# A spectral filter and a GeGLU layer on one core: forward transforms on two 64-row halves of TensorE, filter planes on both partition halves, filter sums made in the inverse's accumulation, and a new order

## The chip, the cores and the metric

The kernel runs on one core of a Trainium2 chip. The core has five engines that run side by side and wait for each other through semaphores: TensorE (matrix products into PSUM), VectorE, ScalarE, GpSimd and SyncE. Sixteen DMA engines move data; transfers are issued from the queue of an engine, here SyncE's and GpSimd's, in the order of that queue. The metric is the device time of one execution in microseconds, from the program's first to its last instruction and what lies around it. Before the change it is 491.61 us, the median of 3 runs (491.15 to 492.12).

## The reference

One sequence of 2,048 rows with 576 features, bfloat16. A spectral filter with a layer norm ahead of it, then a GeGLU layer with another:

```python
def _A_ref(x, w_r, w_i):
    B, S, D = x.shape
    X = rfft2(x.astype(float32), axes=(-2, -1))
    X = X * (w_r + 1j * w_i)          # 2048 x 289 filter
    return irfft2(X, s=(S, D), axes=(-2, -1)).astype(bfloat16)

def _B_ref(x, w_gate, w_up, w_down):  # 576 x 4608, 576 x 4608, 4608 x 576
    return (_gelu(x @ w_gate) * (x @ w_up)) @ w_down

h = x + _A_ref(_layernorm(x), A_w_r, A_w_i)
h2 = h + _B_ref(_layernorm(h), B_w_gate, B_w_up, B_w_down)
```

## The kernel before

There is no transform instruction: each step of the Fourier transform is a matrix product with a table of sines and cosines. The rows are kept as 16 tiles `XO[:, c, :]` of 128 partitions. The work runs in five stages; the order inside the first three is written out by hand as a list of short words, which the builder turns into instructions one after the other, so each engine gets its instructions in the order of the list. `Prog` puts in the semaphore waits from what each instruction reads and writes.

*Stage A* (list `SEQ1`). Statistics of the first layer norm (`B`, `b`, `S`, `Q`, `v`, `q`, `c`), scaled tables `ATS` (`x`, L506 and L511), negated and copied columns of x for the even and odd parts (`n`, `t`: `XN`, L553 and L558), then the first transform over 128 of the 2,048 rows (`M`, `a_mm`, L537) into PSUM, and evictions to `U` (`E`, `F`, L548). `U` holds five column blocks for 16 groups.

*Spectral stage* (list `SEQF`). It works through 16 groups of frequencies, group 1 first, group 0 last (`GORD`). For each group:

- `D` (`st_D`, L611): the transform along the features, six matmuls of 128 rows by 288 columns into two PSUM banks, evicted to `CUS` by ScalarE.
- `B` (`st_B`, L621): the last part of the row transform, four matmuls of 288 columns into two banks, real and imaginary part; evicted to `YS` by ScalarE (L603 is the helper that records all these evictions).
- `T` (`st_T`, L630): VectorE multiplies both parts with both filter planes and a negated one, 4 x 288 products into `TP`.
- `w` (`st_w`, L635): VectorE makes the negated plane, in four pieces.
- `Z` (`st_Z`, L641 and L644): VectorE adds the products pairwise into `ZS` (256 columns) and `ZR` (the 32 columns that remain).
- `V` (`st_V`, L651): the first step of the inverse, four matmuls of 256 columns, evicted to the tile `V` by ScalarE.
- `R` (`st_R`, L663 and L666): the same for the remaining columns, four groups at a time; VectorE multiplies with a mask `MK` into `VR`.

The filter planes lie in `WS`. Partitions 0 to 63 hold the rows of a frequency and 64 to 127 those of its mirror. They come by 22 transfers on SyncE's queue (`w_up`, `w_down`, L441 to L451), the imaginary plane first, with the table `VT` between the two halves; behind them in the same queue come `DT`, `IT`, `DP`, `ITD`, `IDT` and the up weights. The source of a `w_up` steps 16 x 4 x a contiguous run, that of a `w_down` 16 x 8 (or 7) rows of 289 elements, backwards.

*Inverse stage* (list `SEQ`). For the first six tiles, the remaining feature transform (`I`, L736), the row transform (`N`, L779) and the residual (L796), then the second layer norm, transposes (L841) and the first pieces of the GeGLU layer (`g`, `h`). The other ten tiles are done later, between the matmuls of the first down projection (L895, L913).

*GeGLU layer*. Four blocks of 512 rows: gate and up products on two 64-row halves of TensorE (L877), then the down product (L978). The weights for its first quarter are loaded into slot 0 of `WG3`; slots 1 and 2 share memory with `WS`, so their loads wait until the last product `T` is done. The gate half is issued on GpSimd's queue behind all that GpSimd has to do up to there, the up half on SyncE's.

Of the kernel before, what the change touches and what calls it, by code (L numbers as in the profile page):

```python
# [4 lines left out]
BF16 = mybir.dt.bfloat16  # L5
# [5 lines left out]
KW = 288  # L11
HK = 144
NZ = 5
# [10 lines left out]
SEQ1 = """S3 B0 t1 b0 b1 B1 v0 q0 c0 Q3 n0 m3D B2 k14 t0 x0P b2 n1 v1 q1 n2 k104 c1 B5 S4 m4P b5 Q4 B6 M0 E1A b6 v2 B7 x1P E0A M1 E4A q2 E5A t2 b7 c2 B9 E3A x2P E2A E8A E6A b8 S13 B8 b9 v3 q3 k202 M2 B11 B10 n3 n4 c3 x3P E12A b10 b12 E9A b11 B12 v4 E13A Q13 E7A q4 E10A t3 E11A B15 m13P E14A M3 t4 c4 E15A E16A b14 x4P M4 B14 b15 t5 v5 E17D q5 E18A E21A n5 E19A c5 x5D E20D E22D E23A E24A F23A F24A M5 E27A E25D E29A F29A E26D E28D F28A F25D F27D F22A F26D""".split()  # L24
# [3 lines left out]
SEQF = """D0 D1 w0 D2 B0 T0 D3 B1 Z0 D4 T1 Z1 B2 V0 T2 B3 D5 T3 B4 D6 w1 Z2 T4 Z3 D7 B5 D8 w3 B6 w2 D9 T5 Z4 B7 Z5 T6 B8 R0 D11 T7 V2 Z7 D10 V1 B9 T8 B10 D13 Z6 V4 T9 T10 R1 D12 V3 Z8 B11 B12 Z9 D14 T11 V6 B13 T12 V5 B14 Z11 V7 Z10 T13 D15 Z12 T14 V8 Z13 V9 B15 Z14 R2 T15a V12 V10 T15b Z15a V11 Z15b V13 V14 R3 V15 R4""".split()  # L28
VENG = [('act',), ('act',), ('act',), ('act',), ('act',), ('act',), ('act',), ('act',), ('act',), ('act',), ('act',), ('act',), ('act',), ('act',), ('act',), ('act', 'act')]
DENG, BENG = ['act', 'act', 'act', 'act', 'act', 'act', 'act', 'act', 'act', 'act', 'act', 'act', 'act', 'act', 'act', 'act'], ['act', 'act', 'act', 'act', 'act', 'act', 'act', 'act', 'act', 'act', 'act', 'act', 'act', 'act', 'act', 'act']  # L30
SEQ = """I0 I1 N0 I2 s0 N1 I3 S1 q0 N2 I4 c0 e0 s2 q1 n0 n1 N3 I5 c1 z0 n2 s3 e1 D1 N4 N5 e2 q2 c2 n3 e3 D2 g10 g00 h10 z3 h00 g20 g01 h20 h01 g21 g11 h21 h11""".split()
# [14 lines left out]
def build_tables():  # L46
# [39 lines left out]
    fr = np.zeros((6, 128, 2, HK))  # L86
    for o, kk in enumerate((k2o, k2e)):
        for h, fn in enumerate((np.cos, np.sin)):
            for t in range(2):
                fr[3 * o + t, :, h] = fn(ang(np.arange(128 * t, 128 * t + 128), kk))  # L90
            fr[3 * o + 2, 64:96, h] = -fn(ang(np.arange(544, 576), kk))
            fr[3 * o + 2, 96:128, h] = fn(ang(np.arange(256, 288), kk))
# [43 lines left out]
    T["BTAB"] = B.reshape(2, 3, 128, 128).transpose(2, 0, 1, 3).reshape(128, -1)  # L136
    T["VTAB"] = V.reshape(2, 2, 128, 256).transpose(2, 0, 1, 3).reshape(128, -1)
# [175 lines left out]
def _build(nc, A_x, A_w_r, A_w_i, B_w_gate, B_w_up, B_w_down, out):  # L313
# [16 lines left out]
    WS = sb.alloc("WS", [128, 3, NG, K2], BF16)  # L330
# [11 lines left out]
    XN = sb.alloc("XN", [128, NT, 320], BF16)  # L342
# [23 lines left out]
    U = sb.alloc("U", [128, 5, NG, NT, 8], BF16)  # L366
# [7 lines left out]
    FT = sb.alloc("FT", [128, 6, 2 * HK], BF16)  # L374
    BT = sb.alloc("BT", [128, 2, 3, 128], BF16)
    VT = sb.alloc("VT", [128, 2, 2, 256], BF16)
# [4 lines left out]
    assert sb.off <= end1  # L381
# [10 lines left out]
    TP = sb.alloc("TP", [128, 3, 2, 2, KW], BF16)  # L392
    ZS = sb.alloc("ZS", [128, NZ, 2, 256], BF16)
    ZR = sb.alloc("ZR", [128, 2, 2, 128], BF16)

# [42 lines left out]
    def w_up(pl, hf):  # L438
        g0, g1 = ((0, 9), (9, 16))[hf]
        src = (A_w_r, A_w_i)[pl].tensor  # L440
        P.dma(SP, WS[0:64, 1 + pl, g0:g1, :].rearrange("p g k -> p (g k)"), bass.AP(src, g0 * K2, [[128 * K2, 16], [16 * K2, 4], [1, (g1 - g0) * K2]]),  # L441
              f"w{pl}{hf}", w=[("W", hf, pl, 0)])
# [10 lines left out]
    for pl in (1, 0):  # L453
        w_up(pl, 0)
        w_down(pl, 0)
# [593 lines left out]
```

## Time and profile before

The profiled execution took 489.2 us from its first to its last instruction; the median of the runs is 491.61. Busy times and idle times below are of that one execution.

| engine | busy us | share of the span | instructions |
|---|---|---|---|
| TensorE, matmul | 481.8 | 98% | 4,376 |
| TensorE, weight load | 286.3 | 59% | 4,376 |
| VectorE | 193.6 | 40% | 399 |
| ScalarE | 150.7 | 31% | 297 |
| GpSimd | 32.1 | 7% | 60 |

Where it stands in time:

| stage | from, us | to, us |
|---|---|---|
| stage A | 0 | 19.9 |
| spectral stage | 19.9 | 48.3 |
| inverse, second norm, transposes | 48.3 | 57.1 |
| GeGLU, with the last ten inverse tiles inside | 57.1 | 487.3 |

Transfers (of DMA queue records):

| transfer | KB each | issue to landing, us |
|---|---|---|
| FT | 432 | 10.1 |
| BT | 192 | 10.0 |
| WS, eight largest groups | 36 to 325 | 6.1 to 9.6 |
| gate weights | 1,152 | 10.2 |
| output | 72 | 1.6 |

Over the whole span the DMA engines moved 31.2 MB; q1, SyncE's hardware queue, 18.6 MB of it.

How to read it: the busy share of TensorE over the whole span says little about the spectral stage, because the GeGLU layer fills most of the time. What the spectral stage costs is read from that stage alone. In the lines that follow, L611 and the like are lines of the kernel before; an entry such as `x96 | 13.9, 286` is a count, the busy time in us, and the mean time of one in ns. A matmul's recorded time covers its whole way through the array; successive ones overlap, so their spacing, not their mean time, is what they cost TensorE.

### The profile page before, as it was taken

The numbers are of one execution on the slowest core, as the hardware profiler recorded it, in microseconds if no ns is written. First come the engines' busy times: TensorE is split into PE (matmuls) and PEld (weight loads), VectorE is DVE, ScalarE is ACT, GpSimd is POOL, SyncE is SP. The second block draws the span as 40 slices with busy tenths as digits, with TensorE's granted clock in tenths as the row PEclk, the third lists the DMA queues.
The fourth block names the chain that finished last, engine by engine and source line by source line (L and its number), as shares of the span: only waits on it lengthen the run. The fifth ranks groups of instructions, "written<-read, shape, count | busy, mean of one in ns | idle before, by whom it ended". The sixth has DMA issues, their size and how long they took to land.

```text
span 489.2 us, 9939 instructions
## 1 busy us (share of the span) xinstructions
PE 481.8 (98%) x4376; PEld 286.3 (59%) x4376; DVE 193.6 (40%) x399; ACT 150.7 (31%) x297; POOL 32.1 (7%) x60
## 2 busy tenths in 40 slices
PE   7899999999999999999999999999999999999998
PEld 3787754444688744444577644444677544444775
DVE  6799733433576634433311144333211233333111
ACT  6999742233322223323200032233100122323000
POOL 5511441000000020000000000000000000000000
PEclk9999999999999999999999999999999999999999
DMA  8990999100001071100000001000000000000000
GB/s 283 231 325 16 365 366 340 26 15 2 1 19 40 13 233 23 24 4 1 2 18 19 13 20 22 16 0 1 7 19 19 7 1 0 1 2 1 13 20 18
DMA packets 25148, 31.20 MB, mean 64 GB/s; under 512 B 11440, under 2 KB 17840, under 8 KB 25104
## 3 DMA queue, kind: packets, MB, share of 16 engines
q1 hardware_dynamic: 22208, 18.62, 13.4%
q0 software_dynamic: 2896, 11.95, 7.0%
q8 instruction: 34, 0.56, 0.5%
q14 instruction: 10, 0.08, 0.1%
HBM read 26.22 MB, written 2.36 MB: 58 GB/s over the span
## 4 chain that ended last, share of the span: by engine, by line
PE 92%; ACT 3%; DVE 3%; DMA 1%; issue 0%; SPq 0%; POOL 0%; DVEq 0%
PE PS L877 57%; PE PS L978 29%; PE PS L537 1%; DMA XO<-in_A_x_dram 1%; DVE TP L630 1%; PE PS L895 1%; ACT V L603 1%; PE PS L736 1%; ACT YS L603 1%; PE PS L611 1%; PE PS L779 1%; PE PS L913 1%; ACT U L548 0%; DVE VR L666 0%; ACT CUS L603 0%
## 5 line engine op out<-in xcount | busy, mean ns | idle before, releaser
L877 PE MATMUL PS<-HT,WG 64*128 64x512 bf16 (+1 forms) x2160 | 228.7, 371 | 0.0
L877 PEld LDWEIGHTS PS<-HT,WG 64*128 64x128 bf16 x2160 | 105.0, 94 | 121.9 <-issue 0.7
L886 DVE TENSOR_TENSOR AT<-GL,PS 128x512 bf16<-128x512 bf16 (+1 forms) x147 | 99.4, 677 | 177.9 <-ACT GL L885 177.9
L885 ACT ACTIVATE GL<-PS 128x512 bf16<-128x512 f32 (+1 forms) x147 | 86.5, 588 | 262.6 <-PE PS L877 251.3
L978 PE MATMUL PS<-WD,AT 128*128 128x288 bf16 (+2 forms) x1152 | 144.9, 286 | 0.0
L978 PEld LDWEIGHTS PS<-WD,AT 128*128 128x128 bf16 x1152 | 110.7, 98 | 30.6 <-ACT GL L885 0.8
L877 PE MATMUL PS<-HT,WGX 64*128 64x512 bf16 x486 | 53.4, 376 | 0.0
L981 DVE TENSOR_TENSOR OS<-PS,XO 128x288 bf16<-128x288 f32 (+2 forms) x32 | 14.6, 457 | 94.4 <-PE PS L978 94.3
L877 PEld LDWEIGHTS PS<-HT,WGX 64*128 64x128 bf16 x486 | 23.7, 94 | 28.8
L611 PE MATMUL PS<-FT,U 128*128 128x288 bf16 x96 | 13.9, 286 | 0.0
L630 DVE TENSOR_TENSOR TP<-YS,WS 128x1152 bf16<-128x1152 bf16 (+2 forms) x17 | 12.0, 719 | 2.7 <-ACT YS L603 2.5
L900 ACT ACTIVATE EB<-PS 128x288 f32<-128x288 f32 x10 | 4.1, 411 | 27.6 <-PE PS L895 27.6
L537 PE MATMUL PS<-ATS,XO 128*128 128x128 bf16 x96 | 8.6, 219 | 3.1 <-POOL ATS L506 1.6
L480 DVE BATCH_NORM_STATS2 ST<-XO 128x6 f32<-128x288 bf16 x26 | 10.0, 441 | 2.7 <-DMA XO<-in_A_x_dram 2.7
L918 DVE TENSOR_TENSOR XO<-PS,XO 128x576 bf16<-128x576 f32 x10 | 7.6, 756 | 8.0 <-PE PS L913 8.0
L611 PEld LDWEIGHTS PS<-FT,U 128*128 128x128 bf16 x96 | 9.2, 98 | 2.3
L603 ACT ACTIVATE CUS<-PS 128x576 bf16<-128x576 f32 x16 | 10.4, 659 | 0.5 <-PE PS L611 0.3
L603 ACT ACTIVATE YS<-PS 128x576 bf16<-128x576 f32 x16 | 10.3, 664 | 0.4 <-DVE TP L630 0.4
L621 PE MATMUL PS<-CUS,BT 128*128 128x288 bf16 x64 | 10.0, 286 | 0.0
L548 ACT ACTIVATE U<-PS 128x256 bf16<-128x256 f32 (+2 forms) x29 | 9.6, 417 | 0.7 <-PE PS L537 0.6
L906 DVE TENSOR_TENSOR QB<-PS,EB 128x288 f32<-128x288 f32 x20 | 8.2, 452 | 3.3 <-ACT EB L900 3.3
L823 DVE TENSOR_SCALAR HN<-XO,NM,RS 128x576 bf16<-128x576 bf16 (+1 forms) x28 | 9.2, 369 | 0.1
(80 smaller groups left out, 207.6 us busy)
## 6 DMA issues: line engine op xcount, KB each, us to landing
WD<-in_B_w_down_dram POOLq DMA_DIRECT2D x9, 576.0 KB, 12.0
WG<-in_B_w_up_dram SPq DMA_DIRECT2D x4, 1152.0 KB, 7.8
WG<-in_B_w_gate_dram POOLq DMA_DIRECT2D x4, 1152.0 KB, 10.2
out_dram<-OS SPq DMA_DIRECT2D x30, 72.0 KB, 1.6
XO<-in_A_x_dram SPq DMA_DIRECT2D x3, 576.0 KB, 7.4
WGX<-in_B_w_up_dram SPq DMA_DIRECT2D x1, 1152.0 KB, 6.0
WGX<-in_B_w_gate_dram POOLq DMA_DIRECT2D x1, 1152.0 KB, 10.0
HT<-HN SPq DMA_TRANSPOSE x60, 2.4
```

Of the source, the lines that this page charges most:

```text
L480: P.op(DVE, lambda v: v.bn_stats(ST1[:, c, h, :], XO[:, c, 288 * h:288 * h + 288]), r=[("X", c)], w=[("ST1", c, h)])
L537: P.op(PE, lambda t, b=b, lhs=lhs, s=s, e=e, o=o, c=c: t.matmul(bank(b, 0, 128, o, o + 128), lhs, ATS[:, c, :], start=s, stop=e), r=[("X", ...
L548: fn = (lambda v: v.tensor_copy(dst, src)) if eng == DVE else (lambda a: a.activation(dst, src, ACTF.Copy))
L603: fn = (lambda v: v.tensor_copy(dst, src)) if eng == DVE else (lambda a: a.activation(dst, src, ACTF.Copy))
L611: P.op(PE, lambda t, b=b, m=m, us=us, o=o: t.matmul(bank(b, 0, 128, 0, 2 * HK), U[:, us, i, :, :], FT[:, 3 * o + (2 if us == 4 else us // ...
L621: P.op(PE, lambda t, b=b, tb=tb, m=m, s3=s3, sp_=sp_: t.matmul(bank(b, 0, 128, 0, KW), BT[:, sp_, tb, :], CUS[:, s3, m, :], start=(m == 0) ...
L630: P.op(DVE, lambda v: v.tensor_tensor(TP[:, tl, :, :, q0:q1], y4, w4, op=ALU.mult), r=[("Y", sl), ("Wn", i)] + (wkeys[0] if 1 <= g < 9 els ...
L877: op = P.op(PE, lambda t, h0=h0, kt=kt, wt=wt, b=b, s=(not second and j == 0), e=(second and j == n - 1): t.matmul(bank(b, 0, 128, c0, c1) ...
L885: P.op(ACT, lambda a: a.activation(GL[:, s2, c0:c1], bank(b0, 0, 128, c0, c1), ACTF.Gelu_apprx_tanh), r=[("PS", b0)], w=[("GL", s2)])
L886: P.op(DVE, lambda v: v.tensor_tensor(AT[:, f, c0:c1], GL[:, s2, c0:c1], bank(b0 + 1, 0, 128, c0, c1), op=ALU.mult), r=[("GL", s2), ("PS", ...
L978: P.op(PE, lambda t, b=b, d0=d0, d1=d1, f=f, p=p: t.matmul(bank(b, 0, 128, 0, d1 - d0), AT[:, f, 128 * p:128 * p + 128], WD[:, f, d0:d1], ...
L981: P.op(DVE, lambda v, b=b, d0=d0, d1=d1, p=p, c=c: v.tensor_tensor(OS[:, p % 2, d0:d1], bank(b, 0, 128, 0, d1 - d0), XO[:, c, d0:d1], op=A ...
```

## The change

Filter planes. `WS` becomes `[128, 2, 2, NG, K2]`: plane, half `h` of a group's frequencies, group, feature. The 64 rows of a half and the mirror rows now lie on partitions 0 to 63, and the same values once more on 64 to 127. They come in four chunks of groups, each chunk in twelve loads from device memory and then two copies from one partition half to the other; the negated plane is gone.

```diff
-    def w_up(pl, hf):
-        g0, g1 = ((0, 9), (9, 16))[hf]
-        P.dma(SP, WS[0:64, 1 + pl, g0:g1, :]..., bass.AP(src, g0 * K2, [[128 * K2, 16], [16 * K2, 4], [1, (g1 - g0) * K2]]),
...
+    WP = ((1, 5), (5, 9), (9, 16), (0, 1))
+    def w_load(j):
+        g0, g1 = WP[j]
+        n = g1 - g0
+        for pl in range(2):
+            src, nm = (A_w_r, A_w_i)[pl].tensor, f"w{pl}{j}"
+            for h in range(2):
+                P.dma(SP, WS[0:32, pl, h, g0:g1, :].rearrange("p g k -> p (g k)"), bass.AP(src, (g0 + 32 * h) * K2, [[16 * K2, 2], [128 * K2, 16], [1, n * K2]]),
+                      nm, w=[("W", pl, j, h)])
+            for jl in range(2):
+                for h in range(2):
+                    p0, k0 = 32 + 16 * jl, 128 - 32 * h - 16 * jl - g0 - 64 * (g0 + jl + h == 0)
+                    P.dma(SP, WS[p0:p0 + 16, pl, h, g0:g1, :], bass.AP(src, k0 * K2, [[128 * K2, 16], [-K2, n], [1, K2]]), nm, w=[("W", pl, j, 2 + 2 * jl + h)])
+    def w_copy(j):
+        g0, g1 = WP[j]
+        for pl in range(2):
+            P.dma(SP, WS[64:128, pl, :, g0:g1, :]..., WS[0:64, pl, :, g0:g1, :]..., f"v{pl}{j}",
+                  r=[("W", pl, j, i) for i in range(6)], w=[("W", pl, j, 6)])
+    w_load(0)
+    w_load(1)
+    w_copy(0)
+    P.dma(SP, VT...)
+    w_load(2)
+    w_copy(1)
+    w_load(3)
+    w_copy(2)
...
+    w_copy(3)
```

Transforms on halves. `U` is laid out so that the 64 lower and the 64 upper partitions of a `D` product hold two halves of the group. `st_D` makes ten matmuls of 64 rows where it made six of 128, in two passes (`D`, six, and `d`, four), so that each pair works on both halves of TensorE and on two banks; the eviction follows the second pass, on ScalarE or, for six groups, on VectorE. `st_B` makes four matmuls of 64 rows.

```diff
+        for j in range(3 - second):
+            for half in range(2):
+                o = half ^ second
+                us, h0, b = (1 - o, 3 - o, 4)[j], 64 * half, b0 + o
+                ... t.matmul(bank(b, 0, 128, 0, 2 * HK), U[h0:h0 + 64, us, i, ...], FT[h0:h0 + 64, ...], start=(not second and j == 0), stop=(second and j == 1))
...
+        for m in range(2):
+            for half in range(2):
+                h0 = 64 * half
+                ... t.matmul(bank(b0 + half, 0, 128, 0, KW), BT[h0:h0 + 64, sp_, m, :], CUS[h0:h0 + 64, s3, m, :], start=(m == 0), stop=(m == 1))
```

Products and sums. `T` multiplies `YS`, or for four groups (word ending in `x`) the PSUM banks directly, with both planes. The sums of `Z` are gone: `V` and `R` accumulate the products in PSUM, with twice as many matmuls of 128 columns that write every other run of four columns. `Z` is now a copy of the 32 remaining columns of the four products, on GpSimd for ten groups, on VectorE for four, on ScalarE for two. `TP` has six buffers where it had three.

```diff
+        w4 = WS[:, :, :, g, 1:K2].rearrange("p w h k -> p h w k")
+        y4 = y.unsqueeze(2).to_broadcast([128, 2, 2, KW])
+        P.op(DVE, lambda v: v.tensor_tensor(TP[:, tl, :, :, :], y4, w4, op=ALU.mult), r=rk + wkeys[3 if g == 0 else (g > 4) + (g > 8)], w=[("T", tl)])
...
+            for h in range(2):
+                for w in range(2):
+                    ... t.matmul(bank(b, ...).rearrange("p (a s e) -> p a s e", s=2, e=4)[:, :, h, :],
+                                 TP[:, tl, h, w, c:256:2], VT[:, sp_, w, h, :], start=(w == 0), stop=(w == 1))
```

Tables and stage A. `FT` goes from 1,728 to 1,440 elements a partition, `BT` from 768 to 512, `VT` stays at 1,024. `XN` holds 256 columns a tile, and a new tile `XR` of 128 takes the tail columns twice, once from each half. Three of the six groups of `ATS` are now scaled on VectorE, one before.

Order. `SEQ1`, `SEQF` and `SEQ` are new lists. The beginning of the spectral one:

```diff
-SEQF = """D0 D1 w0 D2 B0 T0 D3 B1 Z0 D4 T1 Z1 B2 V0 T2 B3 D5 T3 B4 ..."""
+SEQF = """D0 D2 d0D D1 d2 d1D D3 B0x d3 D4 B1x T0x d4 B2 T1x D5 B3 T2 d5 Z0D D7 T3 B4 ... T14 B15 V11 T15 V10 Z13P Z14D V13 R2 Z15 V14 V12 V15 R4 R3"""
```

The wait of the first gate weight load on GpSimd is now for the second chunk of the planes (`wkeys[1]`). The GeGLU layer's code is as before.

More of the change, by code (lines that the diff above doesn't have):

```diff
@@ L12 @@
 HK = 144
-NZ = 5
+NP = 6
 ABASE = 1
@@ L380, in _build @@
     YB = sb.alloc("YB", [128, D], BF16)
-    assert sb.off <= end1
     v_off = max(end1, sb.off)
@@ L697, in _build @@
     wdv = B_w_down[:, :].rearrange("(c p) d -> p c d", p=128)
-    P.alias(wkeys[0] + wkeys[1] + [("Wn", i) for i in range(NG)], [("WG", j, k) for j in (1, 2) for k in range(4)])
+    P.alias(sum(wkeys, []), [("WG", j, k) for j in (1, 2) for k in range(4)])
     def wg_tile(slot):
```

213 lines of the change are left out of this document (96 added, 117 removed).

## The prediction

> **What bounds the kernel now.** I read four views, in this order: the chain of waits in order of time, the busy time by stretch, the groups of instructions by shape, and the DMA view of the first 30 us.
>
> ```profile
> 24.02 0.75 PE PS L611 x6
> ...
> 45.46 2.74 ACT V L603 x6
> ...
> 48.34 1.63 PE PS L736 x12
> ...
> 56.86 0.28 PE PS L841 x5
> ...
> 58.77 0.03 issue
> 58.81 0.44 PE PS L841 x5
> 59.25 68.58 PE PS L877 x674
> ...
> 170.66 70.04 PE PS L877 x648
> ```
>
> Columns: start, length, what. From 59.25 us on, the chain is TensorE alone, gap by gap closed; the change leaves that code as it is. So the change can only act between 0 and 59 us, and what it shifts there shifts the end one for one. The spectral stage runs from the first L611 (20.1) to the inverse (L736, 48.34), some 28.3 us.
>
> ```profile
> core 0: us, PE busy (x) PEld busy (x) DVE busy (x) ACT busy (x) POOL busy (x), PEclk, DMA share, GB/s
> 25.00:30.00 5.00, 5.00 (x43) 4.04 (x42) 4.75 (x12) 4.89 (x9) 1.54 (x2) 1.00 1.05 377
> 30.00:35.00 5.00, 5.00 (x44) 4.10 (x43) 4.93 (x12) 4.58 (x9) 0.00 (x0) 1.00 1.04 331
> 40.00:45.00 5.00, 5.00 (x45) 4.08 (x43) 4.89 (x15) 5.00 (x11) 0.00 (x0) 1.00 0.01 3
> ```
>
> Three engines are full at once in that stage (clock 1.00), so a gain needs all three relieved. The prices:
>
> ```profile
> L630 DVE TENSOR_TENSOR TP<-YS,WS 128x1152 bf16<-128x1152 bf16 x15 | 11.2, 755 | 2.7 <-ACT YS L603 2.5
> L603 ACT ACTIVATE CUS<-PS 128x576 bf16<-128x576 f32 x16 | 10.4, 659 | 0.5 <-PE PS L611 0.3
> L666 DVE TENSOR_TENSOR VR<-PS,MK 128x1024 bf16<-128x1024 f32 x3 | 3.7, 1219 | 0.0
> ```
>
> And the transfers from 5 to 30 us, in 40 slices of 0.625 us, with the issues of the filter planes on SyncE's queue (ns: least/median/most):
>
> ```profile
> GB/s 295 383 339 276 304 390 397 407 401 433 397 420 279 199 243 222 254 222 219 212 224 208 279 215 226 224 229 201 174 192 293 216 255 386 408 403 402 379 407 379
> ...
> L223 SPq DMA_DIRECT2D WS<-in_A_w_i_dram x11: 552/600/706, 5.7 to 16.1; - x11
> L223 SPq DMA_DIRECT2D WS<-in_A_w_r_dram x11: 595/598/612, 9.1 to 20.0; - x11
> ```
>
> About 400 GB/s until slice 12 (12.5 us: x and tables), then about 220 while the filter planes come in, half of them as rows of 578 B. 400 over 16 DMA engines is 25 GB/s each, 220 is 14. The first filter product (L630) starts at 23.62 and waits for ScalarE, not for these transfers.
>
> **The change part by part: the engines.** TensorE: L611's six matmuls of 288 columns take 0.75, 0.122 each, and L621's the same. L877 shows halves of 64 rows: 70.04/648 = 0.108 for 512 columns, so 0.061 for 288. Forward transforms: 96 x 0.122 = 11.7 before, 160 halves x 0.061 = 9.8 after. B: 64 x 0.122 = 7.8 before, 64 x 0.061 = 3.9 after. The inverse's first step (V, R): 74 x 0.11 of 256 columns before, 148 of 128 columns after; L537 does 128 columns in 0.055, so nothing changes, 8.1. Its output now goes in runs of four; no row has that, bounds 0.055 and 0.11 (as 256 columns), I take the first. Sum 27.7 to 21.8.
>
> The 64-row and 128-row forms alternate eight times in the new order, never in the stage before. Between L877's halves five L841 transposes took 0.44, without such neighbours 0.28: 0.08 a switch, 0.6 in all, on an engine that has room. The Trainium skill (TensorEngine Tiling (Array Packing), Key Properties) says that a switch of tiling drains TensorE; a drain of a whole L877 matmul (371 ns) would make it 3 us, the row says 0.6.
>
> ScalarE (spacing back to back 0.55 for 128x576, 0.46 for V): ten CUS of 16, twelve YS of 16, 16 V, two ZR: 20.0 against 25. VectorE loses the sums ZS (16 x 0.34) and the negated plane (L635, 1.8); sixteen ZR sums become copies, ten on GpSimd, four here. It gains six CUS evictions (0.66, as L796 has for 576 from PSUM) and four products read straight from PSUM: VR needs 1.21 for 1,024 such elements, so 1.36 for 1,152 (bounds 0.67 and 2 x 0.75). Sum: 12 x 0.67 + 4 x 1.36 + 6 x 0.66 + 0.5 + VR 5.0 = 23. Begun at 21, that ends at 44 instead of 48.6, where VectorE's last VR ends now. So the engines alone would give up to 4.6 us.
>
> **The filter transfers.** The products of the first four steps now wait for chunk 0 of the planes, the next four for chunk 1, steps 8 to 14 for chunk 2, the last for chunk 3. Each chunk first comes to partitions 0 to 63 in twelve loads, and then goes by two copies to 64 to 127; SyncE's queue runs load 0, load 1, copy 0, VT, load 2, copy 1, load 3, copy 2, copy 3, and only then DT, IT and the weights. A copy waits in that queue for its chunk's landing, and everything behind it too. 22 issues become 56.
>
> Bytes: the up rows are 2 planes x 2 x 32 partitions x 16 x 578 = 1.18 MB, the down rows as many, and the copies 2.37 MB that did not exist. Now the doubtful point. Every transfer of the profile has 16, 64 or 128 entries in the slowest step of both its sides. The sixteen up loads alone break this: source 2 x 16 x n, destination 32 partitions. If the work is dealt out along that step, two DMA engines carry each up load, the other fourteen none. The bounds are 16 and 2; I take 2, since an equal deal along both outermost steps (2 and 32) allows no more. The Trainium skill (DMA: Bandwidth & Descriptors, "How many engines (k)") says that such a DMA is split by the largest k up to 16 that divides both slowest dimensions, on the lowest-numbered engines. No run shown so far can confirm it.
>
> Then each of these two engines carries, up to copy 2: up rows 592 KB, down rows 74, copies 139, VT 16. Long rows at 25 GB/s: 747/25 = 29.9 us; the 578 B rows at 14: 5.3. They start at 12.1 (12.5 less 136 KB of FT and BT no longer loaded). Queue order gives copy 0 at 12.1 + 11.8 + 2.6 + 1.5 + 1 for landing = 29, chunk 1 at 44, chunk 2 at 12.1 + 35.2 + 1 = 48.3. SyncE's issues (24 x 0.64 to 21.1, the next fourteen to 32) lie before that and cost nothing. The landing of 1 us is from the output stores (1.6 from issue, 0.33 of it issuing).
>
> From 48.3, VectorE still has six products of 0.67, two of 1.36, a ZR copy 0.2 and three VR of 2.5 together: 9.4, in order, so the last VR ends at 57.7 against 48.6. All the engines' savings, and the reordered first stage, are hidden behind the planes: step 0 waits until 29 where stage A ends near 20, and 9 us of cover is there.
>
> GpSimd's issue of the first gate weights moves behind ten ZR copies, the last after the thirteenth product (53.7); landing took 10.2, so 64, and the first use comes at 57.1 + 9.1 = 66. Hidden; without that cover, in a stage that ends as before, it would be 47.2 + 10.2 against 57.1, some 0.3 us. DT and IT go out at about 47 and land some 7 later, before 57.
>
> Sum: 9.1 on the profiled execution's 489.2 is 498.3. The median of the runs shown, 491.61, stands 2.4 above that span, so 500.7, say **501**.
>
> **Rivals.** *Dealt to all 16 engines: the queue bounds.* 2.37 MB at 220 and as much at 400 GB/s take 17 us, done by 30; SyncE is the limit. At 0.64 an issue chunk 2's copies leave at 41 and land at 43.3, the stage ends near 53.7: +5.1, 496.7. With the table loads' issue (0.43 + 0.04) for the 32 short loads, they land at 37.8 and the stage ends at 47.2: -1.4, 490.2. Middle 494. For it: 16 DMA engines were busy on all former loads. Against: none of those had a 2 there.
>
> *No plane is late* (faster): copies pass quickly and issues are short; then the engine sums decide: -4.6 with about half a us of gaps given back, 487.5. For it: three engines lose 3 to 6 us each. Against: 34 more issues on one queue at 0.43 or more are 15 us, and the last copy would have to land by 33.
>
> *Two engines at the crowded rate*: long rows at 14 GB/s too make 821/14 = 58.6 us; chunk 2 lands at 71.7, +32.5, 524. For it: the slices around 220. Against: there all sixteen engines worked on rows of 578 B, here fourteen idle most of the time.
>
> **How the numbers follow.** Forecast 0.62, its own range 496 (everything at 433/16 = 27 GB/s, 30.4 us, +4) to 512 (long rows near 18); queue-bound 0.23; no plane late 0.07; crowded rate 0.08. The range 490 to 511 leaves out the last two and little else. A difference of 0.2% (1 us) can be told from none. Faster: 0.07 plus the low end of the queue case, 0.11. Same: 0.08. Slower: 0.81.
>
> **What would show it.** Right: L652, the changed kernel's product, idles before its steps 0, 4 and 8 until about 29, 44 and 48, its releaser a DMA on WS; the copies of WS land long after issue; GB/s in slices from 14 to 45 us falls below 100, as two engines at 25 give; TensorE shows gaps. The queue case would show gates at 24, 34 and 38 to 43 with SyncE issuing without a pause. Wrong altogether: products back to back from 23 us, and the stage's end at 44. L629 halves above 0.07 each, or V matmuls at 0.11, would show my TensorE prices wrong without moving the sum.

## The result, and the profile after

| | before | after |
|---|---|---|
| median of the runs, us | 491.87 (491.15 to 492.31) | 514.32 (512.52 to 515.15) |
| ratio, 95% interval | 1 | 1.0462 (1.0436 to 1.0487) |
| span of the profiled execution, us | 489.2 | 510.7 |
| first filter product (step 0) starts, us | 23.62 | 33.56 |
| last VR ends, us | 48.6 | 69.8 |
| inverse (I) starts, us | 48.34 | 69.51 |

The change makes the kernel 4.6% slower, and all of it is there before the inverse starts: 69.51 − 48.34 = 21.2 of the 21.5 us. Line numbers are now those of the changed kernel: L234 issues a DMA, L629 is `D`, L642 `B`, L652 the product `T`, L659 `V`, L677 and L680 `R`, L619 an eviction, L748 the inverse, L889 the GeGLU products.

First the page's 40 slices of 12.8 us each. Busy tenths of TensorE, the share of the DMA engines in tenths, and what they moved:

```profile
PE   7824799999999999999999999999999999999998
...
DMA  8533989961000107010000001100000000000000
GB/s 278 126 75 82 244 293 349 372 221 22 1 1 13 33 24 225 20 24 1 1 1 18 17 16 25 22 6 1 1 19 17 13 1 1 1 1 1 13 19 17
```

The third and fourth slice (25.5 to 51 us) show TensorE at 2 and 4 tenths, which was full there before, and 75 and 82 GB/s, where the rows of before had 377 and 331 from 25 to 35 us. Who waits for whom is in VectorE's timeline (start, length, instruction; in brackets how long VectorE had idled and what released it):

```profile
33.56 2.62 DVE L652 TENSOR_TENSOR TP<-PS,WS 128x1152 bf16<-128x1152 f32 x2 [9.79 <-DMA WS<-WS]
...
52.17 1.44 DVE L652 TENSOR_TENSOR TP<-YS,WS 128x1152 bf16<-128x1152 bf16 x2 [11.65 <-DMA WS<-WS]
...
57.83 2.36 DVE L680 TENSOR_TENSOR VR<-PS,MK 128x1024 bf16<-128x1024 f32 x2 [1.35 <-PE PS L677]
60.11 1.46 DVE L652 TENSOR_TENSOR TP<-YS,WS 128x1152 bf16<-128x1152 bf16 x2
...
67.41 2.41 DVE L680 TENSOR_TENSOR VR<-PS,MK 128x1024 bf16<-128x1024 f32 x3
```

Step 0 starts at 33.56 and step 4 at 52.17, each after some 10 us of idling, released by a copy within `WS`. Step 8 starts at 60.11 without waiting for its planes, which had landed at 59.1, a microsecond before VectorE was through with what stands ahead of it. The last VR ends at 69.82. The chain of waits (start, length, what) says the same from the other end:

```profile
29.90 5.95 SPq L234
...
38.03 14.07 DMA WS<-WS
52.17 0.77 DVE TP L652
...
53.67 2.10 PE PS L629 x16
...
60.08 0.61 PE PS L629 x10
...
69.51 1.63 PE PS L748 x12
```

One copy takes 14.07 us from its issue to its landing, and ahead of it SyncE spends 5.95 us in a single issue that has a median of 0.43. And the busy time by stretch, for two stretches in which VectorE waits and for the ten microseconds around steps 4 to 8 (the last three numbers of a row are granted clock, share of the DMA engines, GB/s):

```profile
core 0: us, PE busy (x) PEld busy (x) DVE busy (x) ACT busy (x) POOL busy (x), PEclk, DMA share, GB/s
32.00:33.00 1.00, 0.00 (x0) 0.00 (x0) 0.00 (x0) 0.00 (x0) 0.00 (x0) 0.50 0.13 25
44.00:48.00 4.00, 0.00 (x0) 0.00 (x0) 0.00 (x0) 0.00 (x0) 0.00 (x0) 0.88 0.15 54
...
50.00:55.00 5.00, 1.33 (x12) 0.77 (x14) 2.83 (x5) 1.30 (x2) 0.76 (x1) 0.50 0.59 126
55.00:60.00 5.00, 5.00 (x68) 3.78 (x64) 3.65 (x6) 4.01 (x7) 0.30 (x1) 0.77 0.97 234
```

A share of 0.13 is two engines of sixteen, and some 50 GB/s is what two give at 25 each. (The 25 GB/s of the first row is half of that: the packets of copy 0 and VT that were under way there, of 2,312 and 2,048 B, took about 200 ns each; 94 and 84 ns are their times elsewhere. Why is open.) The trace's records of single packets and landings show the two streams directly. Worked out from them, in us from the span's start (the forecast's column from its own terms: long rows at 25 GB/s, short ones at 14, from 12.1 on, 1 us for a landing; chunk 2's rows are 12.1 + 608/25 + 69/14 + 1, with 608 KB of up rows, copy 0 and VT and 69 of down rows on each of the two engines):

```
landed, us                 forecast   after
load 0                       20.3      21.2
load 1                       27.5      31.0
copy 0                       29        33.5
load 2 (rows of chunk 2)     42.4      50.3
copy 1                       44        52.1
copy 2                       48.3      59.1

marks left by one load of a plane: 70 (before: 80 for five transfers, 16 each)
a packet of 4,046 B: 158 ns in two streams alone, 371 ns (median) from 38 to 42 us
a packet of 2,312 B:  94 ns in two streams alone
```

A load of one plane is six transfers and would leave 6 x 16 = 96 marks on its semaphore. It leaves 70 = 4 x 16 + 2 x 3: the four down loads are carried by sixteen engines, the two up loads leave three marks each. The Trainium skill (DMA: Bandwidth & Descriptors, "How many engines (k)") says that the number of engines must divide the slowest dimension of both sides, here 2 and 32; the trace agrees.

### The profile page after: what moved, and what is told of

Read it like the earlier page. It is cut to its first block, busy times and chain, and to the rows that moved or that the text cites. A ratio compares the mean times of both kernels' runs of the same rounds, so it can differ in the third digit from the quotient of the medians.

```text
span 510.7 us, 10214 instructions
## 1 busy us (share of the span) xinstructions
PE 482.7 (95%) x4513; PEld 283.4 (55%) x4514; DVE 192.1 (38%) x376; ACT 146.7 (29%) x288; POOL 36.7 (7%) x68
## 4 chain that ended last, share of the span: by engine, by line
PE 87%; SPq 7%; DMA 3%; ACT 2%; DVE 1%; issue 1%; DVEq 0%
PE PS L889 55%; PE PS L990 28%; SPq L234 7%; DMA WS<-WS 3%; PE PS L629 1%; PE PS L907 1%; PE PS L659 1%; ACT V L619 1%; PE PS L642 0%; PE PS L925 0%; PE PS L748 0%; DVE XO L808 0%; ACT YS L619 0%; ACT OS L782 0%; ACT GS L619 0%
## 5 line engine op out<-in xcount | busy, mean ns | idle before, releaser
L889 PE MATMUL PS<-HT,WG 64*128 64x512 bf16 (+1 forms) x2160 | 228.7, 371 | 0.0
L889 PEld LDWEIGHTS PS<-HT,WG 64*128 64x128 bf16 x2160 | 104.7, 94 | 122.2 <-issue 0.7
L889 PE MATMUL PS<-HT,WGX 64*128 64x512 bf16 x486 | 53.4, 376 | 0.0
L889 PEld LDWEIGHTS PS<-HT,WGX 64*128 64x128 bf16 x486 | 23.7, 94 | 28.8
L629 PE MATMUL PS<-FT,U 64*128 64x288 bf16 x160 | 15.9, 333 | 19.8 <-DVE TP L652 10.0
L629 PEld LDWEIGHTS PS<-FT,U 64*128 64x128 bf16 x160 | 8.0, 107 | 24.7 <-DVE TP L652 10.3
L619 ACT ACTIVATE YS<-PS 128x576 bf16<-128x576 f32 x12 | 7.7, 657 | 21.4 <-PE PS L642 11.2
L652 DVE TENSOR_TENSOR TP<-YS,WS 128x1152 bf16<-128x1152 bf16 x12 | 9.0, 769 | 12.0 <-DMA WS<-WS 11.7
L554 PEld LDWEIGHTS PS<-ATS,XO 128*128 128x128 bf16 x96 | 6.8, 98 | 5.0 <-POOL ATS L523 2.9
L652 DVE TENSOR_TENSOR TP<-PS,WS 128x1152 bf16<-128x1152 f32 x4 | 5.3, 1348 | 9.8 <-DMA WS<-WS 9.8
## 6 DMA issues: line engine op xcount, KB each, us to landing
WG<-in_B_w_up_dram SPq DMA_DIRECT2D x4, 1152.0 KB, 12.7
```

What stands on the lines that cost most here:

```text
L554: P.op(PE, lambda t, b=b, lhs=lhs, s=s, e=e, o=o, c=c: t.matmul(bank(b, 0, 128, o, o + 128), lhs, ATS[:, c, :], start=s, stop=e), r=[("X", ...
L619: fn = (lambda v: v.tensor_copy(dst, src)) if eng != ACT else (lambda a: a.activation(dst, src, ACTF.Copy))
L629: d_done[i, o] = P.op(PE, lambda t, b=b, us=us, h0=h0, o=o, s=(not second and j == 0), e=(second and j == 1): t.matmul(bank(b, 0, 128, 0, ...
L652: P.op(DVE, lambda v: v.tensor_tensor(TP[:, tl, :, :, :], y4, w4, op=ALU.mult), r=rk + wkeys[3 if g == 0 else (g > 4) + (g > 8)], w=[("T", ...
L889: op = P.op(PE, lambda t, h0=h0, kt=kt, wt=wt, b=b, s=(not second and j == 0), e=(second and j == n - 1): t.matmul(bank(b, 0, 128, c0, c1) ...
```

## The experiments

**1. Sixteen engines for the up rows.** Only the cut of the up loads changes: each takes 16 partitions and both halves h, so that the slowest step of both sides is 16. Same number of transfers, bytes and queue order.

```diff
-            for h in range(2):
-                P.dma(SP, WS[0:32, pl, h, g0:g1, :]..., bass.AP(src, (g0 + 32 * h) * K2, [[16 * K2, 2], [128 * K2, 16], [1, n * K2]]),
+            for jl in range(2):
+                P.dma(SP, WS[16 * jl:16 * jl + 16, pl, :, g0:g1, :]..., bass.AP(src, (g0 + 16 * jl) * K2, [[128 * K2, 16], [32 * K2, 2], [1, n * K2]]),
```

> The up loads of the filter planes are cut the other way: one load for each 16 partitions, both halves h in it, so that source and destination both step 16 first. Number of loads, bytes, order of the queue, copies and all compute stay the same. Theory (an up load whose slowest source step is 2 is carried by two of the 16 DMA engines, which then hold up the copies behind it): the copies of chunk 0, 1 and 2 land near 24, 31 to 34 and 38 to 43 us instead of 33.5, 52.1 and 59.1; SyncE issues without stalls of several us; the stage's last VR ends at 47 to 54 instead of 69.8; time 490 to 497. Rival (the copies between partition halves themselves, and the waits for them in SyncE's queue, are what is slow, however the loads are dealt): chunk 1 still lands after 48 and the time stays above 506.

Measured: 498.80 us (498.06 to 499.63), ratio 1.0146 (1.0128 to 1.0164), just above the 490 to 497 that I expected. So 15.5 of the 22.5 us go with this cut alone, and a load leaves 96 marks. VectorE's timeline again:

```profile
25.55 2.62 DVE L652 TENSOR_TENSOR TP<-PS,WS 128x1152 bf16<-128x1152 f32 x2 [1.68 <-DMA WS<-WS]
...
35.27 1.43 DVE L652 TENSOR_TENSOR TP<-YS,WS 128x1152 bf16<-128x1152 bf16 x2 [3.47 <-DMA WS<-WS]
...
45.69 2.23 DVE L652 TENSOR_TENSOR TP<-YS,WS 128x1152 bf16<-128x1152 bf16 x3 [2.23 <-DMA WS<-WS]
```

The waits have shrunk from 9.8 and 11.7 us to 1.7, 3.5 and 2.2, but there are three, all on copies. The two engines are the main cause; some 7 us have another.

**2. No plane is late.** Four long loads of all 128 partitions, from the memory of the gate weights, stand in for planes and copies; the engines' work is that of the change.

```diff
-        for pl in range(2):
-            src, nm = (A_w_r, A_w_i)[pl].tensor, f"w{pl}{j}"
...
+        P.dma(SP, WS[:, :, :, g0:g1, :]..., bass.AP(B_w_gate.tensor, g0 * K2, [[4 * NG * K2, 128], [NG * K2, 4], [1, n * K2]]),
...
     def w_copy(j):
+        return
```

> The filter is left out: WS is filled by four long loads (one for each chunk, 128 partitions, runs of 4 x 578 B and more) from the memory of the gate weights, as many bytes as loads and copies together, so the products are of other numbers; everything else is the changed kernel. It shows what the engines alone make of the new order. Theory (engine sums 22 for TensorE, 20 for ScalarE, 23 for VectorE from 21 us on): no product waits for a plane after about 25 us, the last VR ends at 44 to 46 against 48.6 before, time 486.5 to 489.5. Rival (the new order, eight changes between 64 and 128 rows on TensorE, and V's output in runs of four are slow by themselves): the last VR ends after 48 and the time is above 491.

Measured: 489.17 us (488.86 to 489.48), ratio 0.9950 (0.9933 to 0.9966). The chain of waits ahead of the first product, and from step 4 to 8 VectorE's timeline:

```profile
21.42 2.02 PE PS L619 x29
...
23.47 0.64 DVE CUS L609
...
24.15 1.37 DVE TP L642
```

```profile
24.15 2.62 DVE L642 TENSOR_TENSOR TP<-PS,WS 128x1152 bf16<-128x1152 f32 x2
...
28.89 1.42 DVE L642 TENSOR_TENSOR TP<-YS,WS 128x1152 bf16<-128x1152 bf16 x2
...
36.78 1.50 DVE L642 TENSOR_TENSOR TP<-YS,WS 128x1152 bf16<-128x1152 bf16 x2
```

The engines are worth 2.6 us by the medians (1.8 by the profiled spans, 489.2 and 487.4), not the 4.6 of my sum. Step 0 starts at 24.15, behind the first 29 half matmuls and an eviction, and not at 21. From step 4 (28.89) to step 8 (36.78) it is 7.9 us. The changed kernel took as long (52.17 to 60.11), but that is a coincidence: it had done part of TensorE's work ahead, while VectorE waited, so that 78 matmuls begin in that stretch of its trace and 130 in this one. On the other hand its granted clock was 0.50 when step 4 began (rows above).

**3. The rate by partitions.** As experiment 2, but chunk 0 comes by loads to 64 partitions, chunk 1 by loads to 16, chunks 2 and 3 by loads to 128; the same source.

```diff
+        for p in range(0, 128, np_):
+            P.dma(SP, WS[p:p + np_, :, :, g0:g1, :]..., bass.AP(B_w_gate.tensor, (4 * p * NG + g0) * K2, [[4 * NG * K2, np_], [NG * K2, 4], [1, n * K2]]),
...
+    w_fill(0, 64)
+    w_fill(1, 16)
...
+    w_fill(2, 128)
+    w_fill(3, 128)
```

> The filter is left out again: WS is filled from the memory of the gate weights with the same runs as in the run with free planes, but chunk 0 by two loads of 64 partitions, chunk 1 by eight loads of 16 partitions, chunks 2 and 3 by one load of 128 partitions each. All go out on 16 engines. Theory (a transfer that touches few partitions is limited at the memory side, not by the number of DMA engines: the run with up loads on 16 engines moved only 120 to 220 GB/s while it filled 16 or 64 partitions at a time): a run of 2,312 B takes near 175 ns in chunk 0 (about 210 GB/s in all) and 300 ns or more in chunk 1 (about 110 GB/s), and a run of 4,046 B in chunk 2 about 160 ns (400 GB/s). Rival (the slow rates come from the 578 B rows, or from odd addresses of the filter in device memory): all three chunks move at 370 to 420 GB/s, 2,312 B in 93 ns.

One run of 490.72 us beside 490.79 before: nothing waits for these loads. The busy time by stretch has loads to 64 partitions in its first row, to 16 mostly in the second, to 128 in the third:

```profile
core 0: us, PE busy (x) PEld busy (x) DVE busy (x) ACT busy (x) POOL busy (x), PEclk, DMA share, GB/s
14.00:18.00 4.00, 3.17 (x49) 2.83 (x48) 3.37 (x16) 3.24 (x10) 3.28 (x6) 0.94 1.04 188
22.00:26.00 4.00, 3.91 (x62) 3.01 (x59) 3.45 (x9) 2.23 (x7) 0.00 (x0) 1.00 1.05 174
28.00:32.00 4.00, 4.00 (x68) 3.10 (x66) 3.77 (x7) 4.00 (x10) 1.85 (x3) 1.00 1.01 398
```

All sixteen engines are busy in each, yet they move 174 to 188 GB/s into 16 or 64 partitions and 398 into 128. The packets of 2,312 B took some 200 to 210 ns into 16 partitions as well as into 64, so the 300 ns that I expected for 16 was wrong. The Trainium skill (SBUF — State Buffer, Door 1: The DMA port swizzle) says that partitions 0 to 63 lie on eight of sixteen ports and measured 196 GB/s there; the trace agrees, with 188. So a transfer into one half of the partitions runs at about half rate when sixteen engines carry it; two engines alone still reach 25 GB/s each (2,312 B in 94 ns). For the copies within `WS` the same is read off other traces: in the changed kernel a packet of 2,312 B of a copy took 94 ns (median) on two engines alone from 49 to 52 us, and 171 ns from 22 to 24 us, with the other fourteen on it; copy 0's last packets, around 32 us, are the exception named above.

**4. Steps over partitions, fewer waits.** Rows permuted so that a load steps over every second partition, sixteen engines, chunks of 5, 4, 4 and 3 groups, one copy for both planes.

```diff
-    WP = ((1, 5), (5, 9), (9, 16), (0, 1))
+    WP = ((0, 5), (5, 9), (9, 13), (13, 16))
...
+                P.dma(SP, WS[jl:32:2, pl, :, g0:g1, :]..., bass.AP(src, (g0 + 16 * jl) * K2, [[128 * K2, 16], [32 * K2, 2], [1, n * K2]]),
...
+                    P.dma(SP, WS[32 + jl:64:2, pl, h, s0:g1, :], bass.AP(src, (128 - 32 * h - 16 * jl - s0) * K2, [[128 * K2, 16], [-K2, g1 - s0], [1, K2]]), ...)
```

> A version meant to be fast, same result: rows of the planes permuted so that each load of 16 partitions steps over every second partition of 32 (tables permuted to match), up loads on 16 engines as in the first experiment, group 0 with the first chunk, the other two chunks of four and three groups, one copy for both planes: 54 issues and 2.37 MB of copies remain. Theory (partitions limit the rate, engines and issues don't): loads at about 210 GB/s, the copies of chunks 0 to 3 land near 23, 30, 35 and 38 us, the last VR ends at 46.5 to 48, time 489 to 491.5, a little below before. Rival (loads to 16 partitions are slow however they are spread, or copies and their waits in the queue are the limit): chunk 2 lands after 40, time 493 to 499.

Measured: 504.48 us (503.90 to 504.98), ratio 1.0273 (1.0257 to 1.0289), worse than experiment 1, against what I expected. SyncE's issues say much of why (ns: least/median/most). First this run, then experiment 1:

```profile
L234 SPq DMA_DIRECT2D WS<-in_A_w_i_dram x25: 592/595/1317, 10.5 to 45.2; - x25
```

```profile
L234 SPq DMA_DIRECT2D WS<-in_A_w_i_dram x24: 420/426/1696, 8.8 to 36.8; - x24
```

An issue takes 0.595 us where it took 0.43, so fifty of them are some 8 us more of one queue, and the last load leaves at 45.2 instead of 36.8. What in the permuted form makes an issue dearer wasn't taken apart, nor what the other chunks and the single copy add.

**5. No copies, the two engines kept.** The changed kernel, with each copy replaced by a load of the same size from the memory of the gate weights, at the same place of the queue, waiting for nothing; the filter's upper half is left out so.

```diff
-            P.dma(SP, WS[64:128, pl, :, g0:g1, :]..., WS[0:64, pl, :, g0:g1, :]..., f"v{pl}{j}",
-                  r=[("W", pl, j, i) for i in range(6)], w=[("W", pl, j, 6)])
+            P.dma(SP, WS[64:128, pl, :, g0:g1, :]..., bass.AP(B_w_gate.tensor, (2 * pl * NG + g0) * K2, [[4 * NG * K2, 64], [NG * K2, 2], [1, n * K2]]), f"v{pl}{j}",
+                  w=[("W", pl, j, 6)])
```

> The changed kernel with its up loads on two engines, but the copies between partition halves are replaced, at the same places of the queue, by loads of as many bytes from the memory of the gate weights into partitions 64 to 127, which wait for nothing; the upper half of the filter is left out so. Theory 1 (the two engines' own rows set the gates; copies slow them only because they stand behind them): chunk 1's last piece still lands after 47, time 509 to 514. Theory 2 (what the forecast missed are the copies: their rate, the waits for them in the queue, and the up rows that slow down from 158 to some 400 ns while copies run): chunk 1 lands at 42 to 46 and chunk 2 near 48 to 51, as the forecast had it, time 501 to 507.

Measured: 514.06 us (513.56 to 515.63), ratio 1.0474 (1.0454 to 1.0495): no gain, as theory 1 has it. VectorE's timeline:

```profile
35.66 2.62 DVE L653 TENSOR_TENSOR TP<-PS,WS 128x1152 bf16<-128x1152 f32 x2 [11.49 <-DMA WS<-in_B_w_gate_dram]
...
54.02 1.43 DVE L653 TENSOR_TENSOR TP<-YS,WS 128x1152 bf16<-128x1152 bf16 x2 [11.55 <-DMA WS<-in_B_w_gate_dram]
```

So neither the read of the lower half nor SyncE's wait for a landing is what costs. The other transfer of the same size does as much harm: the upper half of chunk 1 was complete 1.4 us after chunk 2's rows (52.5, then 53.9), as a sixteenth of it stands behind them on each of the two engines, and the rows themselves came even later than the 50.3 of the changed kernel.

**6. The two engines with nothing beside them.** The changed kernel's loads, but the upper half is written by GpSimd, as five copies in its own order.

```diff
+    PC = ((1, 5, 0), (5, 9, 1), (9, 13, 2), (13, 16, 2), (0, 1, 3))
+    def p_copy(c):
+        g0, g1, j = PC[c]
+        P.op(POOL, lambda g: g.tensor_copy(WS[64:128, :, :, g0:g1, :]..., WS[0:64, :, :, g0:g1, :]...),
+             r=[("W", pl, j, i) for pl in range(2) for i in range(6)], w=[("W", 2, c)])
```

> The changed kernel with its loads as they are (two engines carry the up rows), but the eight copies by DMA are replaced by five copies that GpSimd makes as instructions (XN's rows show GpSimd at 0.83 us for 768 elements, so 5.0 us for a piece of four groups, 4,624 elements on 64 partitions), placed in GpSimd's order before the ZR copies that need them. Nothing else runs on the DMA engines beside the up rows but the down rows and VT. Theory 1 (the two engines lost some 7 us of the changed kernel's 38 between 12 and 50.3 because the copies on the other fourteen engines slowed their rows): the rows of chunk 2 land at 42 to 44 instead of 50.3, step 4 starts near 35 and step 8 at 48 to 50, the last VR ends near 59, time 501 to 504. Theory 2 (the time was lost because SyncE's queue stalled and left the two engines without work, or the rows are simply that slow): chunk 2 lands at 48 or later, step 8 at 53 or later, time 506 or more.

Measured: 506.77 us (506.52 to 507.01), ratio 1.0316 (1.0297 to 1.0334). GpSimd's timeline shows when the rows are there:

```profile
22.47 4.03 POOL L466 COPY WS<-WS 64x4624 bf16<-64x4624 bf16 x1 [1.91 <-DMA WS<-in_A_w_i_dram]
31.64 4.05 POOL L466 COPY WS<-WS 64x4624 bf16<-64x4624 bf16 x1 [5.13 <-DMA WS<-in_A_w_i_dram]
...
46.27 4.04 POOL L466 COPY WS<-WS 64x4624 bf16<-64x4624 bf16 x1 [8.39 <-DMA WS<-in_A_w_i_dram]
50.44 0.29 POOL L616 COPY ZR<-TP 128x128 bf16<-128x128 bf16 x1
```

Chunk 2's rows land at 46.2, between the two theories. That is 4.1 us earlier than with DMA copies. But without copy 0's share (37/25 = 1.5 us) the forecast's terms give 40.9, so 5.3 us are missing with no copy at all, and the copies add 2.6 beyond their share. The packet records show where: on each of the two streams the up rows of chunks 0 to 2 took 29.5 us, and at 94 and 158 ns they would have taken (256 x 0.094 + 128 x 0.158)/2 = 22.1. The slow ones lie beside other work: the last tables up to 15 us, and bursts of down rows on all sixteen engines (thirteen rows of 4,046 B at 230 to 730 ns from 33.9 to 37). The stall of theory 2 isn't there, although SyncE was held for up to 5.9 us in an issue: between 12 and 46 us there were at no time fewer than two packets under way. Up rows pause twice for some 0.9 us, at 30 and 38.5, but down rows and VT's packets run in these pauses. The up rows are 7.4 us longer and yet 5.3 are missing, because the down rows took less than the forecast gave them (31 ns for 578 B, not 41). The time came out above theory 1's for one more reason: the ZR copy that the next R needs stood behind GpSimd's 4.04 us piece until 50.44, and step 8 started at 52.65.

**7. Sixteen engines and GpSimd's copies.** The cut of experiment 1 and GpSimd's pieces of experiment 6, at the same places of the hand-written order:

```diff
-SEQF = """D0 D2 d0D ... Z1P Z2 ... Z3P B7 Z4P d10D ... Z7P V4 ...
+SEQF = """P0 P1 D0 D2 d0D ... Z1P Z2 ... Z3P B7 Z4P P2 d10D ... Z7P P3 V4 ...
```

> Up loads cut so that sixteen engines carry them (as in the run that did that alone, 498.8 us), and the DMA copies replaced by GpSimd's own copies, 5.0 us for four groups by XN's row. Theory 1 (the 7 us that remained there are the copies: 2.37 MB more through the DMA engines, and SyncE's waits in front of them): chunk 0's loads land at 18 to 20, GpSimd copies until 24.5, 29.5, then 35 and 39, so the first product starts at 24 to 25, step 4 at 29 to 30, step 8 at 36 to 38, and the time is 488.5 to 491, not slower than the kernel before. Rival (the loads alone are the limit, 48 issues on SyncE and rows to 16 partitions; or GpSimd's copies are much slower beside VectorE's work): step 8 at 42 or later, time 494 to 499.

Measured: 495.03 us (494.29 to 495.58), ratio 1.0074 (1.0061 to 1.0087). The planes were in time (load 2 landed at 31.2, load 3 at 33.3), as theory 1 has it, but the time is the rival's, and step 8 started at 42.16. VectorE's timeline, then GpSimd's:

```profile
27.54 2.17 DVE L649 TENSOR_TENSOR TP<-YS,WS 128x1152 bf16<-128x1152 bf16 x1
...
34.34 3.19 DVE L649 TENSOR_TENSOR TP<-YS,WS 128x1152 bf16<-128x1152 bf16 x1
```

```profile
25.05 4.05 POOL L466 COPY WS<-WS 64x4624 bf16<-64x4624 bf16 x1 [0.15 <-POOL WS L466]
...
32.89 4.04 POOL L466 COPY WS<-WS 64x4624 bf16<-64x4624 bf16 x1 [0.16 <-POOL ZR L616]
```

A product of two bf16 operands in SBUF takes 0.75 us; the one that starts at 34.34, during GpSimd's copy, takes 3.19, and the one at 27.54, during the copy that ends at 29.1, takes 2.17. Both end some 0.6 us after the copy: VectorE waits until it is over (the products read from PSUM are not held up: 2.62 for two, as in experiment 2). The Trainium skill (SBUF — State Buffer, Who interferes with whom) says that a product with both inputs in SBUF and a GpSimd instruction that reads SBUF exclude each other for a whole instruction; the trace agrees. These two collisions are 1.4 and 2.4 of the 5.4 us by which step 8 comes after that of experiment 2; the rest wasn't taken apart.

**8 and 9. Copies as DMAs in another order.** Both with sixteen engines, one copy for both planes, and chunk 2 cut in two (9 to 13, 13 to 16). In the first, the copies are issued on GpSimd's queue; in the second, on SyncE's.

```diff
-    WP = ((1, 5), (5, 9), (9, 16), (0, 1))
+    WP = ((1, 5), (5, 9), (9, 13), (13, 16), (0, 1))
...
+    def p_copy(j, eng=POOL):
+        P.dma(eng, WS[64:128, :, :, g0:g1, :].rearrange("p a h g k -> p (a h) (g k)"), WS[0:64, :, :, g0:g1, :].rearrange("p a h g k -> p (a h) (g k)"), f"v{j}",
```

> Sixteen engines carry the up loads; the copies are DMAs again, one for both planes, but issued on GpSimd's queue, which is idle from 20.5 us on, with the large chunk cut in two (9 to 13, 13 to 16). SyncE then never waits for a landing. Theory (what remained at 498.8 us is the order of one queue: a copy stands behind the loads of the next chunk and SyncE stalls ahead of it, while the bytes as such fit: 2.37 MB at about 170 GB/s and as much at 208 are 25.4 us, from 12.2 to 37.6): copy 0 lands near 24, copy 1 near 28, the next near 33 and 38, step 4 starts at 29 to 30 and step 8 at 37 to 39, time 488.5 to 491.5. Rival (the bytes bind: each copy also slows the loads behind it, whatever the queue): step 8 at 41 or later, time 493 to 498.

> The same loads, chunks and merged copies, all on SyncE's queue as in the changed kernel. 60 loads of 0.43 us and five copies of 0.64 with gaps make some 33 us of issues from 5.8 on, before any stall. If the order of the one queue is what binds, this run stays near the run with sixteen engines alone (495 to 499) whatever the run on two queues does; if only the size of the large chunk bound there (its copies took 7.7 us), step 8 starts at 40 and the time is 492 to 493.5.

Measured: 501.24 us (499.41 to 501.70), ratio 1.0211 (1.0197 to 1.0225), and 502.98 (501.69 to 503.20), ratio 1.0238 (1.0223 to 1.0253). Both are misses: slower than experiment 1, and than both of my theories. VectorE's timeline of each:

```profile
42.33 1.47 DVE L648 TENSOR_TENSOR TP<-YS,WS 128x1152 bf16<-128x1152 bf16 x2
...
52.85 0.76 DVE L648 TENSOR_TENSOR TP<-YS,WS 128x1152 bf16<-128x1152 bf16 x1 [3.98 <-DMA WS<-WS]
```

```profile
44.18 2.23 DVE L653 TENSOR_TENSOR TP<-YS,WS 128x1152 bf16<-128x1152 bf16 x3 [0.44 <-DMA WS<-WS]
...
53.03 0.76 DVE L653 TENSOR_TENSOR TP<-YS,WS 128x1152 bf16<-128x1152 bf16 x1 [5.36 <-DMA WS<-WS]
```

Step 8 comes a little earlier than in experiment 1 (45.69), but a wait appears behind it, for the last chunks: twelve more loads are 12 x 0.47 (0.43 and a gap) = 5.6 us more of SyncE's queue, which ends its loads at 44.0 and 46.8 instead of 37.2. With the copies on a queue of their own, their packets (4,624 B in 365 ns, 12.7 GB/s an engine) still pass through the same sixteen engines as the loads. Bytes and issues may both bind; these two runs don't part them.

**10. GpSimd's copies, half as long.** Experiment 7 with the planes copied as 32-bit elements, in four pieces instead of five (groups stored from 1 on, so that the pieces begin at even elements).

```diff
+    PC = ((0, 4, (0,)), (4, 8, (1,)), (8, 12, (2,)), (12, 16, (2, 3)))
+    WF = [WSF[64 * u:64 * u + 64, :].bitcast(F32).rearrange("p (x y) -> p x y", x=4) for u in range(2)]
...
+        c0, c1 = s0 * K2 // 2, s1 * K2 // 2
+        P.op(POOL, lambda g: g.tensor_copy(WF[1][:, :, c0:c1], WF[0][:, :, c0:c1]),
```

> The run with sixteen engines and GpSimd's own copies (495.0 us), where two products that began during a copy took 2.17 and 3.19 us instead of 0.75 and ended with the copy. Here the same bytes are copied as half as many 32-bit elements, in four pieces (groups stored from 1 on, group 0 last, so that pieces begin at even elements). Theory 1 (GpSimd's time goes by elements, 0.87 ns each, and VectorE's bf16 products wait for as long as a copy runs): a piece takes about 2.0 us instead of 4.03, the first two are over before step 2, step 0 starts near 24.2, step 4 at 29, step 8 at 37 to 38, span 487.5 to 489, time 489 to 491: level with the kernel before or up to 0.4% faster. Rival (time goes by bytes): pieces stay at 4 us and the time at 494 to 496.

Measured: 490.40 us (489.59 to 490.80, 12 runs) beside 490.96 before (17 runs), ratio 0.998 (0.997 to 0.999). GpSimd's timeline, then VectorE's:

```profile
20.65 2.11 POOL L471 COPY WS<-WS 64x2312 f32<-64x2312 f32 x1 [0.16 <-POOL NM L594]
22.91 2.11 POOL L471 COPY WS<-WS 64x2312 f32<-64x2312 f32 x1 [0.15 <-POOL WS L471]
...
32.10 2.69 POOL L471 COPY WS<-WS 64x2312 f32<-64x2312 f32 x1 [1.64 <-DMA WS<-in_A_w_i_dram]
```

```profile
24.14 2.61 DVE L654 TENSOR_TENSOR TP<-PS,WS 128x1152 bf16<-128x1152 f32 x2
...
28.88 1.42 DVE L654 TENSOR_TENSOR TP<-YS,WS 128x1152 bf16<-128x1152 bf16 x2
...
32.06 0.75 DVE L654 TENSOR_TENSOR TP<-YS,WS 128x1152 bf16<-128x1152 bf16 x1
...
33.40 2.00 DVE L654 TENSOR_TENSOR TP<-YS,WS 128x1152 bf16<-128x1152 bf16 x1
...
38.00 1.47 DVE L654 TENSOR_TENSOR TP<-YS,WS 128x1152 bf16<-128x1152 bf16 x2
```

A piece takes 2.11 us instead of 4.04, the first two are over before the product that collided, and steps 0 and 4 start as in experiment 2. One collision is left: the product at 33.40 takes 2.00 us, 1.25 too long, and step 8 starts 1.2 us after experiment 2's. The copy seems to have waited in its turn: it began at 32.10, while the product of 32.06 was running, and took 2.69 us, 0.6 more than the others. This is the change with its transfers mended, and it is 0.1 to 0.3% faster than the kernel before.

## Why the prediction was right or wrong

The direction and the mechanism were right: the up loads are dealt to two engines, step 0 and step 4 wait for copies, and the end shifts by what the last VR shifts. The time is 13.6 us above 500.7 and 3 above the range. The runs settle the account: 514.3 becomes 498.8 with sixteen engines, 490.4 with the copies off the DMA engines too, and 489.2 with no plane late at all (the kernel before beside them: 491.0 to 491.9).

- *Two engines.* Right, by 70 marks, two streams of packets, and 15.5 us in experiment 1.
- *The rows' prices.* Right for a stream alone: 158 ns for 4,046 B is 25.6 GB/s, the forecast had 25; the 578 B rows took 31 ns (18.6 GB/s, forecast 14).
- *"Then each of these two engines carries, up to copy 2 ... 35.2": the step that failed.* It added up the rows as if the two engines worked undisturbed, and charged a copy no more than its share on these two. Chunk 2's rows landed at 50.3, not 42.4, and copy 2 at 59.1, not 48.3. By experiment 6, 5.3 of the first 7.9 us are there without any copy (up rows slowed beside tables and down rows), and 2.6 come with the copies, beside which a row of 4,046 B took 371 ns. The other 2.9 us lie between the rows and copy 2, 8.8 us where the forecast had 5.9: with sixteen engines on copy 2, its packets of 4,046 B took some 310 ns, half of the rate that I had put in. I had weighed the crowded rate as a rival (524) and put it aside because "fourteen idle most of the time"; the truth lies between.
- *The gates.* The forecast let step 8's planes (48.3) decide, 4.3 us after step 4's. In the run step 4 started at 52.17 (copy 1 at 52.1 against 44), and step 8 7.94 us later, 1.0 after its planes. That microsecond is the clock's, by an estimate from the rows above: with 0.50 granted, the first sixteen half matmuls took 2.10 us, 0.131 each, where ten at full clock take 0.61, so these sixteen alone were 1.1 us longer for it; VectorE idled 1.35 us for TensorE ahead of VR, and 1.1 us less of that would have had it ready at 59.0, when the planes came. No run tests this. So the planes of step 8 nearly decided, as forecast.
- *The sum.* 10.8 (copy 2), 1.0 and 0.3 (the tail, 9.7 against 9.4) are the 12.1 us by which the last VR's end exceeds 57.7; the span exceeds 498.3 by 12.4. The median stands 3.6 above the profiled span, not 2.4, as the execution profiled was the fastest of the four.
- *SyncE's issues "cost nothing".* They took up to 5.95 us each, not 0.64, and copy 1, whose chunk was there at 31.0, left at 37.3 to 38. In the changed kernel this is hidden, since it would have stood behind chunk 2's rows on the two engines anyway; that is argued from the order of the queue, no run shows it.
- *The engines' gain.* 2.6 us (1.8 by the spans) instead of 4.6 (experiment 2). VectorE's sum "begun at 21" overlooked what its own row said: the first product before started at 23.62, because it waits for `D`, its eviction and `B`. The cover ahead of the planes is therefore 24.15 less some 20, about 4 us, not 9. TensorE's prices held at full clock: ten L629 halves in 0.61 us are 0.061 each, as forecast, and 32 V matmuls in 1.95 us (experiment 2) are 0.061 each, against 0.055. The 0.6 us for switches of tiling can't be told apart in any run, and the rows that I read it from don't give it: in the chain of the kernel before, five L841 transposes take 0.44 us at 54.94 and at 55.44 too, with no 64-row matmul beside them.
- *The queue-bound rival* (490 to 496.7) is what experiment 1 makes real, at 498.8, above its upper end. I had the copies at 400 GB/s; from 38 to 42 us of that run, with a copy on all sixteen engines, a packet of 4,046 B took 310 ns, half of that rate. How much of the remaining 7 us this is, and how much the order of the queue, no run parts.

## What to carry to other kernels

Look at the slowest dimension of both sides of a transfer before its bytes: a 2 in front left fourteen of sixteen DMA engines out and cost 15.5 us, and cutting the same transfer the other way was free. A copy into half of the partitions by DMA can be paid three times: in the queue that waits for it, in the engines that it shares with the loads, and in a rate that is half. Here GpSimd, which had little else to do, made the copies instead, and the time fell by some 8 us. When a sum of work on a shared resource sets a gate, price it with the neighbours that run at the same time, and then see whether the work behind the earlier gate, at the clock that TensorE has after idling, doesn't already cover the later one.

## What the runs showed of the hardware that I had not expected

- Sixteen busy DMA engines move 174 to 188 GB/s into 16 or 64 partitions and 398 into 128 (experiment 3), and an engine with the others idle is no faster than 25.6 GB/s.
- A copy from 64 partitions to 64 others ran at 4,046 B in 310 ns, 13 GB/s an engine, with all sixteen on it (experiment 1, 38 to 42 us); on two engines alone its packets reached 25 GB/s (2,312 B in 94 ns, changed kernel, 49 to 52 us).
- GpSimd's copy costs by elements, not by bytes: 4.04 us for 4,624 elements of 16 bits, 2.11 for 2,312 of 32 bits. While it runs, VectorE's products of two operands in SBUF stand still, and the one copy that began during such a product took 0.6 us longer (experiments 7 and 10).
- An issue on SyncE took 0.43 us in one form and 0.595 in another, and up to 5.95 in the changed kernel, while two engines were behind with their rows.
- TensorE's granted clock fell to 0.50 in and after idle stretches of the changed kernel (32 to 33 and 50 to 55 us, above), and half matmuls then took 0.131 us instead of 0.061. At step 8 this cost about 1 us by the estimate above; elsewhere it was hidden behind the planes.
